# Attention and ResMLP on one core: lam products and beta1 of the first pair on VectorE, and two W1 blocks cast in DRAM beforehand

## The chip, the cores and the metric

The kernel runs on one core of a Trainium2 chip. The metric is device time in microseconds (us) of one execution. An execution that was profiled stands beside the plain runs; its trace gives every instruction's start and duration. Engines are named as in the profile: PE is TensorE (PEld its weight loads), DVE is VectorE, ACT is ScalarE, POOL is GpSimd, SP is SyncE, which here only issues DMAs.

## The reference

Eight batches of 384 tokens. Attention has 16 query heads and 4 key and value heads of 64; its output, laid side by side, is x of width 1024. Then a ResMLP block with affine layers:

```
scores = q k^T / 8 ; attn = softmax(scores) ; x = attn v           (8 x 384 x 1024)
a1  = alpha1 * x + beta1
tok = w_tok @ a1               (384 x 384, over the tokens of a batch)
u   = x + lam * tok
a2  = alpha2 * u + beta2
ch  = relu(a2 @ w_ch1) @ w_ch2         (1024 -> 4096 -> 1024)
out = u + lam * ch
```

All tensors are float32 in DRAM; the matmuls take bfloat16.

## The kernel before

Batches go in four pairs. A pair (`pair`, L772) has two products. The **first product** is a2 times w_ch1, the **second** the hidden layer times w_ch2. Both are done with seven block products in place of eight, in Strassen's manner, numbered o = 1 to 7: sums of blocks of a2 (`sums_a`, L446), of w_ch1 (`sum_w1`, L506) and of w_ch2 (`sum_w2`, L496) are made on VectorE. The w_ch2 sums are made once, during the first pair, and stored to DRAM as bfloat16 (`w2s`, by `keep_w2`, L493, on SP); later pairs fetch them. W1 blocks are loaded anew in every pair by `load_w1` (L181), as casting DMAs from GpSimd's queue into a ring of six slots (`w1`); the same ring holds W2 blocks in the second product. `queue` with `pump` (L534) issues loads in a fixed order as slots come free. `order1` is the order of the W1 blocks, 0, 8, 1, 9, 2, 10 and so on.

While TensorE does the second product of a pair, the attention and token mixing of the next two batches is woven in. `side(b)` (L214) gives these pieces; `put` (L1071) writes into a plan which piece follows which step of which product, and `steps` runs it. A step is a yield of the product, in the second product after every four matmuls. So the order of instructions on each engine is written out by hand. For each of 8 head pairs p of a batch, `side` does scores (L260) and exp (L269), then attention times v with 1/sum and alpha1 on VectorE (L300, L303, L309), then token mixing on TensorE (`tok`, L324), then u = x + tok (L331) and alpha2 (L334) on VectorE. Finally a2 is transposed: in batch 3 and part of others by TensorE (`turn`, L398) with a copy on ScalarE (L400), otherwise by a DMA on SP.

There are two ways of adding beta1. With `fold` (batches 0 to 3) an extra matmul of two stored rows, R and H, is added to every token tile (L328). R and H lie in the memory of the vector `h1` (L97). Without `fold` (batches 4 to 7), VectorE multiplies by alpha1 into a float32 tile `a1f` (L312) and adds lam * beta1 from `h1` (L313). `h1` is set up by `rows4_on` (two memsets on GpSimd, two small loads on SP), `to_all` (a shuffle on VectorE, L1037) and `scale_beta` (a product, L1040), put into the first product of the second pair (steps 20 to 76).

The second product's results are multiplied by lam (`scaled`, L788) and added to the output in DRAM by an accumulating DMA of GpSimd's queue (`store`, L442). The multiplication is L790: on GpSimd for the first pair (`lead`), on VectorE for the others. The first pair's second product is `second_product` (matmuls L752, copies of sums on ScalarE L744 and L764, sums on VectorE L767). Later pairs' first products are L831, their second products L897.

In the first pair, W2 blocks lie for a while in `home(c)` (L468), four places in `arena` that later hold the hidden layer.

Of the kernel before, what the change touches and what calls it, by code (L numbers as in the profile page):

```python
# [13 lines left out]
def kernel(  # L14
# [21 lines left out]
    nc = tc.nc  # L36
    f32 = mybir.dt.float32
    bf = mybir.dt.bfloat16
    EXP = mybir.ActivationFunctionType.Exp
    RELU = mybir.ActivationFunctionType.Relu  # L40
    MUL = mybir.AluOpType.mult
# [8 lines left out]
    P = 128  # L50
    NST = S // P
    NDT = DM // P
# [4 lines left out]
    CW = 2  # L57
    NCH = NNT // CW
    RING = 6
# [21 lines left out]
    w1 = const.tile([P, RING, NDT, CW * P], bf, tag="w1", name="w1")  # L81
# [3 lines left out]
    g1, h1, al2, lam_t = (vecs[:, i] for i in range(4))  # L85
# [10 lines left out]
    turn, a2_turn = [0], [0]  # L96
# [20 lines left out]
    snaps = hTf.bitcast(f32)  # L117
    SLOTS = 7 * NH // 4
    w2s = [tc.dram_tile([P, NDT * CW * P], bf, name=f"w2s{i}") for i in range(SLOTS)]
    PLACE2 = {o: i for i, o in enumerate((1, 2, 6, 5, 3, 7, 4))}  # L120

    def by_tok(ap):
# [53 lines left out]

    w1src = moe_w_ch1.rearrange("(dt di) nf -> di dt nf", di=P)
    w2src = moe_w_ch2.rearrange("(nt ni) d -> ni nt d", ni=P)
    w1_slots, w1_free = {}, list(range(RING))

    def load_w1(c):  # L181
        w1_slots[c] = w1_free.pop(0)
        nc.gpsimd.dma_start(out=w1[:, w1_slots[c]], in_=w1src[:, :, c * CW * P:(c + 1) * CW * P])  # L183

    def bank(shape, tag, name, dtype=f32):
        if tag == "mm":
# [27 lines left out]
    def side(b):  # L214
        vb = vt[b % 2]
        ess, avs, a1s, a2s, xr = {}, {}, {}, {}, {}
        first, fold = b < 2, b < 4
        kT_, qT_ = kTs.get(b, kT), qTs.get(b, qT)

        def x_of(p):  # L220
# [184 lines left out]
        at = {}  # L405

        def put(k, *m):
            at.setdefault(k, []).append(m)
# [3 lines left out]
        for p in range(NP):  # L412
            put((4, 10, 14, 18, 24, 29, 33, 35)[p], av, p)
            put((8, 15, 17, 22, 27, 32, 36, 38 if b % 2 else 39)[p], tok_flip, p)
            if by_pe(p):
                put(((13, 20, 22, 28, 34, 37, 40, 42) if b == 3 else (0, 0, 0, 0, 0, 36, 39, 41))[p], turn, p)
        return at

    def loads(b):
# [19 lines left out]
    order1 = [c for g in range(NCH // 2) for c in (g, g + NCH // 2)]  # L439
# [28 lines left out]
    def home(c):  # L468
        return arena[:, HOME + c * 2048:HOME + (c + 1) * 2048]
# [5 lines left out]
    def stored(c):  # L475
        return w2s[4 * PLACE2[2] + c]

# [26 lines left out]
        free(raw["12", c][0])  # L504

    def sum_w1(g, o):  # L506
        a, c = w1[:, w1_slots[g]], w1[:, w1_slots[g + NCH // 2]]
        H1, H2 = slice(0, NDT // 2), slice(NDT // 2, NDT)
        if o == 7:
            tt(out=c[:, H1], in0=c[:, H2], in1=c[:, H1], op=SUB)  # L510
            tb[g, 7], tb[g, 1], tb[g, 2], tb[g, 3] = c[:, H1], a[:, H1], a[:, H2], c[:, H2]
            return
        tb[g, o] = t = piece().rearrange("p (a c) -> p a c", a=NDT // 2)
        x, y = {5: (c[:, H1], a[:, H1]), 6: (c[:, H2], tb.get((g, 5))), 4: (a[:, H2], tb.get((g, 6)))}[o]
        tt(out=t, in0=x, in1=y, op=SUB)
# [14 lines left out]
    def free(slot):  # L530
        (w1_free if slot < RING else pad_free).append(slot)
        pump()
# [39 lines left out]
    queue = [(load_block, kind, gp) for kind, gp in (("R1", 0), ("R2", 0), ("L1", 1), ("L2", 1), ("R1", 1), ("R2", 1))]  # L572
    queue += [(load_w2, "21", c, w1_free) for c in range(4)]
    for name, cs, slots in (("12", (0, 1), w1_free), ("12", (2, 3), pad_free), ("22", (0,), pad_free), ("22", (1, 2, 3), w1_free),
                            ("again", (0,), w1_free), ("again", (1,), pad_free), ("again", (2, 3), w1_free)):
        queue += [(load_w2, name, c, slots) for c in cs]
    queue += [(load_w1, c) for c in order1[:4]]
    for i in range(1, NB):
        heads = [(load_w1, c) for c in order1[:4]] if i + 1 < NB else []
        queue += [(load_w1, c) for c in order1[4:]] + [(fetch, i, n) for n in range(SLOTS - 2)] + heads[:2]  # L580
        queue += [(fetch, i, n) for n in (SLOTS - 2, SLOTS - 1)] + heads[2:]

    IDENT = mybir.ActivationFunctionType.Identity
# [188 lines left out]
    def pair(i):  # L772
        b0 = 2 * i
        lead = i == 0
# [12 lines left out]

        def scaled(o, b, ms, dw, t):  # L788
            if o != 2 or not last:
                (nc.gpsimd if lead else nc.vector).tensor_tensor(out=t, in0=t, in1=lam_t[:, dw * 512:(dw + 1) * 512], op=MUL)  # L790
            store(b, ms, dw, t)

        def flush(n=9):
# [24 lines left out]
        for g in range(NH // 2):  # L818
            X, Y, snap = {}, {}, {}
            for k, (o, e) in enumerate(SEQ1):  # L820
                t = 2 * g + e
                lo, hi = bias1[:, t:t + 1], bias1[:, NH + t:NH + t + 1]
                if o == 1:
                    X[e] = pairs["X"].tile([P, 512], f32, tag="X", name="X", bufs=2)
                if o == 7:
                    Y[e] = pairs["Y"].tile([P, 512], f32, tag="Y", name="Y", bufs=2)
                if o == 2:
                    Z = pairs["Z"].tile([P, 512], f32, tag="Z", name="Z", bufs=4)
                ps = (X[e] if o in (1, 6, 5, 3) else Y[e] if o in (7, 4) else Z)[:, :S]
                for dt in range(NDT // 2):  # L830
                    nc.tensor.matmul(out=ps, lhsT=tb[g, o][:, dt, e * P:(e + 1) * P], rhs=opb(LEFT1[o])[:, dt],  # L831
                                     start=(o in (1, 2, 7) and dt == 0), stop=(dt == NDT // 2 - 1), skip_group_check=True)
                if o in (1, 6, 5):
                    q = ((2 if g % 2 else 8) + 2 * (1, 6, 5).index(o) + e) % 12 * S
                    snap[o, e] = snaps[:, q:q + S]
                    nc.scalar.activation(out=snap[o, e], in_=ps, func=IDENT, bias=hi if o == 5 else lo)  # L836
                if o == 5:
                    tt(out=hid[:, t, 1], in0=Y[e][:, :S], in1=snap[5, e], op=ADD)  # L838
                elif o == 2:
                    tt(out=hid[:, t, 0], in0=ps, in1=snap[1, e], op=ADD)  # L840
                elif o == 3:
                    nc.scalar.activation(out=hid[:, t, 4], in_=ps, func=RELU, bias=hi)  # L842
                elif o == 4:
                    tt(out=hid[:, t, 2], in0=ps, in1=snap[6, e], op=ADD)
                if k == 7 and 0 < g < 4:
                    flush(1)
                if (o, e) in ((2, 1), (3, 1)):
                    free(w1_slots.pop(g if o == 2 else g + NCH // 2))
                if k == 3 and g == 0:
                    tt(out=opb(6), in0=opb(4), in1=opb(5), op=SUB)  # L850
                if k == 2 and g == 0:
                    sum_w1(0, 4)
                if k in (2, 5, 8, 11) and g + 1 < NH // 2:
                    sum_w1(g + 1, {2: 5, 5: 7, 8: 6, 11: 4}[k])
                ts = slice(2 * g, 2 * g + 2)
                if k == 1 and g:
                    finish(slice(2 * g - 2, 2 * g))
                if (o, e) == (3, 1):
                    nc.scalar.activation(out=hid[:, ts, 1], in_=hid[:, ts, 1], func=RELU)
                if (o, e) == (4, 1):  # L860
                    nc.vector.tensor_scalar(out=hid[:, ts, 2], in0=hid[:, ts, 2], scalar1=0.0, scalar2=None,
                                            op0=mybir.AluOpType.max)
                    tt(out=hid[:, ts, 3], in0=hid[:, ts, 2], in1=hid[:, ts, 1], op=ADD)
                yield 0
# [11 lines left out]
        for k, o in enumerate(PLACE2):  # L876
            whole = not last and o != 4
            tail = last and o == 4
            for h in range(1 if whole else 2):
                for ms in range(NST - (tail and not h)):  # L880
# [37 lines left out]
                    if (whole or h == 1) and not (last and o == 4):  # L918
# [3 lines left out]
                        else:  # L922
                            bb, dw = where[o]
                            t = snap[1, ms] if o == 7 else spare(ms).bitcast(f32)
# [22 lines left out]
    with tc.manual_schedule(engines=order):  # L947
# [123 lines left out]
        def put(ps, phase, at, *m):  # L1071
            plan.setdefault((ps, phase, at), []).append(m)
# [17 lines left out]
        put(0, 0, 8, rows4_on, (3, 0), (3, 1))  # L1090
        put(0, 0, 30, to_all, 3, 0, 0)
        put(0, 0, 34, to_all, 3, 1, 1)
        put(1, 0, 20, rows4_on, (1, 0), (1, 1))
        put(1, 0, 54, to_all, 1, 0, 0)
        put(1, 0, 68, to_all, 1, 1, 1)
        put(1, 0, 62, scale_beta, 0)
        put(1, 0, 76, scale_beta, 1)
        for c in range(4):
            put(0, 0, (50, 72, 74, 44)[c], load_w2, "11", c)
            put(0, 0, (6, 14, 42, 46)[c], cast_w2, "21", c)  # L1100
            put(0, 1, (41, 43, 45, 47)[c], keep_w2, 1, c)
            put(0, 1, 38 + 2 * c, keep_w2, 3, c)
            put(0, 1, (9, 10, 13, 15)[c], sum_w2, 5, c)
            put(0, 1, (20, 21, 25, 26)[c], sums_first_hid, 2, c)
            put(0, 1, (28, 30, 31, 34)[c], sums_first_hid, 4, c)
            put(0, 1, (37, 40, 41, 43)[c], sum_w2, 6, c)
            put(0, 1, (44, 45, 49, 50)[c], sums_first_hid, 3, c)
            put(0, 1, (51, 54, 57, 58)[c], sum_w2, 7, c)
            put(0, 1, (61, 64, 68, 71)[c], last_w2, c)
        for u, o in ((77, 5), (79, 7), (81, 6)):  # L1110
            put(0, 1, u, sum_w1, 0, o)
        for ps in range(NB - 1):
            c = 2 * ps + 2
# [23 lines left out]
        first = steps(0)  # L1137
# [76 lines left out]
```

## Time and profile before

| what | value |
|---|---|
| median of 3 runs | 733.9 us |
| lowest, highest | 733.42, 741.46 us |
| the profiled execution | 731.92 us, its span 729.9 us |
| TensorE busy | 717.4 us (98%), granted clock 1.00 |
| VectorE, ScalarE, GpSimd busy | 543.9, 373.8, 199.2 us |
| moved by DMA | 153.26 MB, mean 210 GB/s |

The span is the time from the first instruction of the trace to the last; the profiled execution's own time is 2.0 us longer. The first pair's first product ends near 128 us, its second product near 234.5 us, and the second pair's first product near 306 us.

How to read the lines: a timeline line is start, duration, engine, line of the kernel, operation, output <- inputs, shape, count, and in brackets how long the engine had been idle before it and what ended that idle. A line of a source view gives minimum, median and maximum duration in ns, and the first and last start. "out<-in" are the program's names: `sc` a PSUM bank of scores or token mixing, `C` an accumulator of the second product, `xr` attention output, `vecs` the vectors lam, alpha and beta, `w` the ring.

### The profile page before, as it was taken

What the parts mean: (1) busy time and instruction counts of PE and PEld (TensorE: products, weight loads), DVE (VectorE), ACT (ScalarE), POOL (GpSimd) and SP (SyncE); (2) the same over time, 40 slices, a digit from 0 to 9 for tenths busy, and PEclk for the clock granted to TensorE, in tenths of its full rate; (3) what the DMA queues carried; (4) which work ended last, traced back from release to release, by engine and by line L of the source; (5) the groups of instructions that cost most, each with busy time, mean ns of one, the idle gap of its engine ahead of it and who ended that gap; (6) DMA issues with size and microseconds to landing.
All of it is one profiled execution on the core that took longest, in us unless ns stands there. A gap on an engine that the chain in (4) does not pass through costs nothing.

```text
span 729.9 us, 14511 instructions
## 1 busy us (share of the span) xinstructions
PE 717.4 (98%) x5716; PEld 408.7 (56%) x5716; DVE 543.9 (75%) x1009; ACT 373.8 (51%) x566; POOL 199.2 (27%) x242
## 2 busy tenths in 40 slices
PE   8899999999999999999999999999999999999998
PEld 4665555555555666555555566655555566654444
DVE  7888876577888988649678888748868988763354
ACT  7877666544563666643433466663333366650000
POOL 8844233221046551201022344200002222000011
PEclk9999999999999999999999999999999999999999
DMA  9999999999999999969989999998989999937965
GB/s 164 180 239 231 190 195 227 226 242 235 366 312 232 179 182 196 234 221 207 272 193 220 160 162 194 212 227 201 270 233 183 210 126 146 165 123 264 302 174 104
DMA packets 197616, 153.26 MB, mean 210 GB/s; under 512 B 90540, under 2 KB 175892, under 8 KB 197292
## 3 DMA queue, kind: packets, MB, share of 16 engines
q0 software_dynamic: 109872, 64.47, 65.4%
q1 hardware_dynamic: 86988, 87.42, 42.8%
q8 instruction: 44, 0.72, 0.4%
q10 hardware_dynamic: 688, 0.46, 0.2%
q14 instruction: 24, 0.20, 0.1%
HBM read 155.23 MB, written 39.85 MB: 267 GB/s over the span
## 4 chain that ended last, share of the span: by engine, by line
PE 90%; DVE 4%; POOL 2%; DMA 1%; issue 1%; ACT 1%; DVEq 0%; ACTq 0%; POOLq 0%
PE C L897 30%; PE X L831 17%; PE C L752 10%; PE Y L831 9%; PE Z L831 4%; PE sc L260 4%; PE X L681 4%; PE sc L295 3%; PE sc L324 3%; PE Y L681 3%; DMA ops<-obuf 1%; DVE pad L565 1%; PE Z L681 1%; PE tok L324 1%; POOL obuf L334 0%
## 5 line engine op out<-in xcount | busy, mean ns | idle before, releaser
L897 PE MATMUL C<-w,arena 128*128 128x512 bf16 (+2 forms) x744 | 168.3, 372 | 0.0
L269 ACT ACTIVATE es<-sc 128x1024 bf16<-128x1024 f32 x108 | 104.1, 1024 | 116.0 <-PE sc L260 107.6
L897 PEld LDWEIGHTS <-arena 128*128 128x128 bf16 x1040 | 94.8, 98 | 100.5 <-issue 5.1
L442 POOL DMA_DIRECT2D out_dram<-hT x45 | 40.0, 888 | 294.7 <-DVE hT L790 135.9
L836 ACT ACTIVATE hT<-X,bias 128x384 f32<-128x384 f32 x144 | 83.6, 582 | 60.0 <-PE X L831 55.2
L831 PEld LDWEIGHTS <-w 128*128 128x128 bf16 x768 | 75.1, 98 | 50.0
L831 PEld LDWEIGHTS <-pad 128*128 128x128 bf16 x576 | 56.4, 98 | 37.2
L183 POOL DMA_DIRECT2D w<-in_moe_w_ch_dram x48 | 45.4, 1002 | 105.6 <-PE X L831 36.5
L831 PE MATMUL X<-ops,w 128*128 128x384 bf16 x384 | 70.3, 326 | 0.0
L831 PE MATMUL X<-ops,pad 128*128 128x384 bf16 x384 | 70.3, 326 | 0.0
L897 PE MATMUL C<-pad,arena 128*128 128x512 bf16 (+2 forms) x296 | 70.2, 373 | 0.0
L324 PEld LDWEIGHTS <-wtokT 128*128 128x128 bf16 x576 | 39.0, 98 | 16.4 <-issue 3.4
L752 PEld LDWEIGHTS <-arena 128*128 128x128 bf16 x336 | 29.8, 98 | 30.0 <-issue 2.5
L331 DVE TENSOR_TENSOR xr<-sc,xr 128x384 f32<-128x384 f32 x48 | 26.5, 553 | 25.6 <-PE sc L324 14.3
L752 PE MATMUL C<-w,arena 128*128 128x512 bf16 x168 | 41.2, 379 | 0.0
L838 DVE TENSOR_TENSOR arena<-Y,hT 128x384 bf16<-128x384 f32 x48 | 26.5, 556 | 17.7 <-ACT hT L836 16.0
L295 PEld LDWEIGHTS <-es 128*128 128x128 bf16 x864 | 32.8, 97 | 11.3
L831 PE MATMUL Y<-ops,w 128*128 128x384 bf16 x192 | 39.1, 326 | 0.0
L831 PE MATMUL Z<-ops,w 128*128 128x384 bf16 x192 | 39.0, 326 | 0.0
L269 ACT ACTIVATE hT<-sc 128x1024 bf16<-128x1024 f32 x36 | 35.8, 1031 | 4.3 <-PE sc L260 4.0
L260 PE MATMUL sc<-qT,kT 64*128 64x384 bf16 (+2 forms) x504 | 37.2, 271 | 0.5 <-ACT hT L269 0.2
L842 ACT ACTIVATE arena<-X,bias 128x384 bf16<-128x384 f32 x48 | 27.9, 582 | 17.7 <-PE X L831 16.1
(190 smaller groups left out, 1175.1 us busy)
## 6 DMA issues: line engine op xcount, KB each, us to landing
w<-w2s SPq DMA_DIRECT2D x67, 512.0 KB, 5.1
w<-in_moe_w_ch_dram POOLq DMA_DIRECT2D x65, 512.0 KB, 9.8
pad<-w2s SPq DMA_DIRECT2D x25, 512.0 KB, 6.9
out_dram<-hT POOLq DMA_DIRECT2D x45, 256.0 KB, 7.1
out_dram<-xr SPq DMA_DIRECT2D x48, 192.0 KB, 5.3
q_raw<-in_q_dram POOLq DMA_DIRECT2D x28, 192.0 KB, 9.5
w2s<-w SPq DMA_DIRECT2D x10, 512.0 KB, 7.6
arena<-in_moe_w_ch_dram POOLq DMA_DIRECT2D x8, 512.0 KB, 15.9
```

The source lines that it names most:

```text
L183: nc.gpsimd.dma_start(out=w1[:, w1_slots[c]], in_=w1src[:, :, c * CW * P:(c + 1) * CW * P])
L260: nc.tensor.matmul(out=sc[:, hh, k % 4:k % 4 + n], lhsT=kT_[r, 2 * p // G, BLK[hh][sk], :], rhs=qT_[r, p, st:st + n, :], start=True, stop= ...
L269: nc.scalar.activation(out=e, in_=sc, func=EXP, scale=scale_qk)
L295: nc.tensor.matmul(out=av[:, hh, sq, :], lhsT=ess[k // 4][:, m % 2, k % 4, :], rhs=vb[:, sk, hk, :], start=(sk == 0), stop=(sk == NST - 1))
L324: nc.tensor.matmul(out=ps[:, tt, :], lhsT=wtokT[:, st, tt * P:(tt + 1) * P], rhs=a1s[p][:, st, :], start=(st == 0), stop=(st == NST - 1 an ...
L442: nc.gpsimd.dma_start(out=by_tok(out[b])[:, ms, dw * 512:(dw + 1) * 512], in_=o, accum_op=ADD)
L681: nc.tensor.matmul(out=ps[:, :n], lhsT=tb[G, o][:, dt, e * P:(e + 1) * P], rhs=opb(FIRST1[o], n)[:, dt], start=(o in (1, 2, 7) and dt == 0 ...
L752: nc.tensor.matmul(out=x, lhsT=lead_hid[:, t, FIRST2[o], ms * P:(ms + 1) * P], rhs=rhs[:, t % 4 * 512:(t % 4 + 1) * 512], start=(o in (1, ...
L831: nc.tensor.matmul(out=ps, lhsT=tb[g, o][:, dt, e * P:(e + 1) * P], rhs=opb(LEFT1[o])[:, dt], start=(o in (1, 2, 7) and dt == 0), stop=(dt ...
L836: nc.scalar.activation(out=snap[o, e], in_=ps, func=IDENT, bias=hi if o == 5 else lo)
L842: nc.scalar.activation(out=hid[:, t, 4], in_=ps, func=RELU, bias=hi)
L897: nc.tensor.matmul(out=x, lhsT=hid[:, t, LEFT2[o], ms * P:(ms + 1) * P], rhs=rhs[:, t % 4 * 512 + c0:t % 4 * 512 + c1], start=((not last o ...
```

## The change

Four edits in one.

1. `fold` holds only for batches 0 and 1. Batches 2 and 3 take the way of L312 and L313. So beta1's preparation moves from the second pair's first product to the first pair's first product: `rows4_on` at step 40, shuffles at 54 and 64, products with lam at 59 and 69.
2. The lam products of the first pair (L790, 12 of them) go from GpSimd to VectorE.
3. Two blocks of the second pair's W1 (`order1[3]` and `order1[4]`) are cast from DRAM to DRAM by GpSimd's queue during the second product (steps 15 and 17), and loaded by SP into `home(0)` and `home(1)` at steps 76 and 77. The ring takes `order1[:3]` there, and the queue goes on with `order1[5:]`.
4. In batch 3 the turn of head pair 2 is put at 23 in place of 22, behind the token mixing of head pair 3.

```diff
+    w1s = [tc.dram_tile([P, NDT * CW * P], bf, name=f"w1s{i}") for i in range(2)]
...
-    w1_slots, w1_free = {}, list(range(RING))
+    w1_slots, w1_at, w1_free = {}, {}, list(range(RING))
...
     def load_w1(c):
         w1_slots[c] = w1_free.pop(0)
-        nc.gpsimd.dma_start(out=w1[:, w1_slots[c]], in_=w1src[:, :, c * CW * P:(c + 1) * CW * P])
+        w1_at[c] = w1[:, w1_slots[c]]
+        nc.gpsimd.dma_start(out=w1_at[c], in_=w1src[:, :, c * CW * P:(c + 1) * CW * P])
+
+    def cast_w1(i, c):
+        nc.gpsimd.dma_start(out=w1s[i].rearrange("p (a c) -> p a c", a=NDT), in_=w1src[:, :, c * CW * P:(c + 1) * CW * P])
+
+    def back_w1(i, c, at):
+        w1_at[c] = at.rearrange("p (a c) -> p a c", a=NDT)
+        nc.sync.dma_start(out=at, in_=w1s[i])
+
+    def free_w1(c):
+        if c in w1_slots:
+            free(w1_slots.pop(c))
...
-        first, fold = b < 2, b < 4
+        first = fold = b < 2
...
-                put(((13, 20, 22, 28, 34, 37, 40, 42) if b == 3 else (0, 0, 0, 0, 0, 36, 39, 41))[p], turn, p)
+                put(((13, 20, 23, 28, 34, 37, 40, 42) if b == 3 else (0, 0, 0, 0, 0, 36, 39, 41))[p], turn, p)
...
-        a, c = w1[:, w1_slots[g]], w1[:, w1_slots[g + NCH // 2]]
+        a, c = w1_at[g], w1_at[g + NCH // 2]
...
-    queue += [(load_w1, c) for c in order1[:4]]
+    queue += [(load_w1, c) for c in order1[:3]]
...
-        queue += [(load_w1, c) for c in order1[4:]] + [(fetch, i, n) for n in range(SLOTS - 2)] + heads[:2]
+        queue += [(load_w1, c) for c in order1[4 if i > 1 else 5:]] + [(fetch, i, n) for n in range(SLOTS - 2)] + heads[:2]
...
-                (nc.gpsimd if lead else nc.vector).tensor_tensor(out=t, in0=t, in1=lam_t[:, dw * 512:(dw + 1) * 512], op=MUL)
+                nc.vector.tensor_tensor(out=t, in0=t, in1=lam_t[:, dw * 512:(dw + 1) * 512], op=MUL)
...
-                    free(w1_slots.pop(g if o == 2 else g + NCH // 2))
+                    free_w1(g if o == 2 else g + NCH // 2)
...
-        put(1, 0, 20, rows4_on, (1, 0), (1, 1))
-        put(1, 0, 54, to_all, 1, 0, 0)
-        put(1, 0, 68, to_all, 1, 1, 1)
-        put(1, 0, 62, scale_beta, 0)
-        put(1, 0, 76, scale_beta, 1)
+        put(0, 0, 40, rows4_on, (1, 0), (1, 1))
+        for i in range(2):
+            put(0, 0, 54 + 10 * i, to_all, 1, i, i)
+            put(0, 0, 59 + 10 * i, scale_beta, i)
...
+        for i, u in enumerate((15, 17)):
+            put(0, 1, u, cast_w1, i, order1[3 + i])
+            put(0, 1, 76 + i, back_w1, i, order1[3 + i], home(i))
```

In the second and later pairs the W1 blocks of a pair come as before.

## The prediction

> **What bounds the kernel now.** I read the page first, for who is busy, then the busy time by stretch, then TensorE's own timeline for the places where it stands still, and last the VectorE and GpSimd timelines around those places.
>
> ```profile
> PE 717.4 (98%) x5716; PEld 408.7 (56%) x5716; DVE 543.9 (75%) x1009; ACT 373.8 (51%) x566; POOL 199.2 (27%) x242
> ```
> ```profile
> 128.00:200.00 72.00, 72.00 (x692) 40.14 (x691) 52.00 (x82) 38.47 (x51) 13.30 (x13) 1.00 1.12 265
> 200.00:235.00 35.00, 33.22 (x299) 18.48 (x298) 31.23 (x49) 18.19 (x29) 16.68 (x16) 1.00 1.15 280
> 235.00:306.00 71.00, 71.00 (x439) 42.76 (x437) 57.46 (x102) 47.50 (x80) 31.44 (x38) 1.00 1.38 191
> ```
>
> TensorE is busy 717.4 of 729.9 us, at a granted clock of 1.00, so 12.5 us of stall is all there is beyond taking matmuls away. Columns of the stretches: length, then busy time of PE, PEld, DVE, ACT, POOL, clock, DMA share, GB/s. 128 to 235 us is the first pair's second product, which carries attention and token mixing of batches 2 and 3; 235 to 306 is the next pair's first product. TensorE loses 1.78 us in 200 to 235 and nothing in the two neighbours. There VectorE is 31.23 of 35 busy, and GpSimd is busiest too.
>
> ```profile
> 204.89 0.33 PE L324 MATMUL sc<-a,wtokT 128*128 128x128 bf16 x3 [0.59 <-ACT es L269]
> ...
> 221.20 0.33 PE L398 MATMUL sc<-ident,obuf 128*128 128x128 bf16 x3 [0.24 <-ACT es L269]
> ...
> 224.76 0.34 PE L324 MATMUL sc<-a,wtokT 128*128 128x128 bf16 x3 [0.95 <-DVE a L309]
> ```
>
> These three idles are the 1.78 us. The last waits for VectorE's alpha1 product of one head pair.
>
> ```profile
> 212.16 0.56 DVE L331 TENSOR_TENSOR xr<-sc,xr 128x384 f32<-128x384 f32 x1 [0.77 <-PE sc L328]
> 212.75 1.77 DVE L334 TENSOR_TENSOR obuf<-xr,vecs 128x384 bf16<-128x384 f32 x1
> ...
> 220.87 2.02 DVE L499 TENSOR_TENSOR w<-w,pad 128x2048 bf16<-128x2048 bf16 x1
> ...
> 225.44 1.74 DVE L309 TENSOR_TENSOR a<-xr,vecs 128x384 bf16<-128x384 f32 x1
> ```
> ```profile
> 212.82 1.28 POOL L790 TENSOR_TENSOR hT<-hT,vecs 128x512 f32<-128x512 f32 x1
> ...
> 220.24 1.55 POOL L790 TENSOR_TENSOR hT<-hT,vecs 128x512 f32<-128x512 f32 x1
> ...
> 225.19 1.56 POOL L790 TENSOR_TENSOR hT<-hT,vecs 128x512 f32<-128x512 f32 x1
> ```
>
> L334 and L309 usually take 0.56 us and L499 1.22. Whenever one overlaps a lam product on GpSimd (L790) it ends about when that product ends: 1.77, 2.02, 1.74 us. Each such meeting costs VectorE 0.4 to 1.2 us.
>
> ```profile
> L328 PE MATMUL sc<-vecs x48: 218/219/219, 138.3 to 227.9; 128*128 128x128 bf16 x48
> ...
> L312 DVE TENSOR_TENSOR a1f<-xr,vecs x32: 557/558/561, 313.9 to 572.7; 128x384 f32<-128x384 f32 x32
> L313 DVE TENSOR_TENSOR a<-a1f,vecs x32: 557/557/559, 314.5 to 573.3; 128x384 bf16<-128x384 f32 x32
> ...
> 238.07 0.69 DVE L515 TENSOR_TENSOR pad<-w 128x1024 bf16<-128x1024 bf16 x1 [2.92 <-DMA w<-in_moe_w_ch_dram]
> ```
>
> The 48 matmuls of L328 go away. L312 and L313 show, from batches 4 to 7, what comes instead. The last line is the wait that the two early casts address: 2.92 us of VectorE, while TensorE is 71.00 of 71 busy.
>
> **The change, part by part.**
>
> *beta1 on VectorE.* Removed: 48 matmuls (L328). Pipelined they are 0.055 us apart: a token group of 12 starts at 138.12 and is followed at 138.79 (0.67 us), one of 9 without them in a later pair at 317.23 and 317.73 (0.50). So 16 x 0.17 = 2.7 us leave TensorE, all of it on the path. Added: 16 VectorE operations; a pair L312, L313 starts 0.59 apart, so 16 x 0.59 = 9.4 us. VectorE has 20.0 us idle in 128 to 200, and I followed its queue there: the operand is ready 1.0 to 2.9 us ahead of its token matmuls for batch 2 still. It costs nothing there except at one place (step 53, near 197 us), where it was just in time: 0.2 us.
>
> *beta1's preparation moved* from the next pair's first product into the first pair's. On VectorE two shuffles of 0.72 (L1037) and two products of 512 columns (0.68, L790's VectorE rows). Two of the four fall in VectorE idles of 2.1 to 2.2 us ahead of L693 and cost nothing; without that cover they would cost their 0.6. Two fall ahead of L702, which frees a Y bank: it ended about 91.6 us where TensorE took the bank at 91.98, 0.4 us to spare against 0.6 added. So 0.25 each, 0.5 in all (bounds 0 and 1.4, their whole time). Two memsets on GpSimd (1.11 us for both) and two 8 KB DMAs on SP move along, into a 5.8 us idle of GpSimd; nobody behind them is near its due time.
>
> *lam products on VectorE.* Twelve of 0.68, queued 0.61 apart: three by 165 us, six in 212 to 230, three beside the next product. GpSimd's queue then holds only stores and loads. Against the six, 3.7 us, stand the meetings that end: 1.21 (L334), 0.37 and 0.52 (L309), 0.80 (L499), 1.18 (L309), together 4.1 us. The Trainium skill ("SBUF — State Buffer", Who interferes with whom) says that a VectorE instruction with two SBUF inputs is blocked by a GpSimd instruction that reads SBUF, not by one that only writes it, and infers that making DMA descriptors needs the write side alone. By that, what stays on GpSimd's queue would hold VectorE nowhere, and the sum is as below; were the stores to hold it too, as in the second rival, it would come out at 735.0. The trace bears the first half (L331, with one PSUM input, is never over 0.56 in 200 to 235); the second half it leaves open.
>
> *VectorE in 204 to 235.* At 204.10 its L499 waits for the landing of a W2 store, which itself hangs on SP's stores, issued without a break from 183 to 206 at 360 to 376 GB/s. TensorE is 1.1 us ahead by then (1.6 less the 0.5 above), but that train is set by DMA, so I take a landing at 203.5, between 203.0 (all shifted) and 204.1 (unmoved). From there the work to the next product's sums was 25.2 us, with 2.0 of idle and 4.1 of meetings: 19.1 of work. Add 4 x 0.58 for beta1, 5 x 0.61 for products, and about 0.2 of waits for ScalarE that stay: 24.6, so the first W1 sum starts at 228.1 (before 229.27). The sums up to the last opb(0) took 5.3 us, one product among them makes 5.9: 234.0. TensorE wants opb(0) for its fifth group of the new product (o=7) at 235.68 in the old count; with 2.7 + 0.6 + 0.2 saved (the last two below), less 0.5 for the preparation and 0.5 for three small waits on VectorE (0.2 above, 0.2 near 208, 0.1 near 224), it would be there at 233.2. It waits 0.8 us: a new stall in a place that had none (bounds 0 and 1.4, by the landing).
>
> *turn of pair 2 of batch 3 one step later.* The 0.59 us at 204.89 is the second score bank being emptied; the turn that took the first bank ahead of it is moved behind it, so the token group takes the bank that is free first: minus 0.6 (bounds 0 and 0.6). The 0.95 at 224.76 falls to about 0.75, the 0.24 stays.
>
> *W1 casts.* Two blocks (order1[3] and [4]) are cast by GpSimd's queue near 146 and 152 us and come back by SP near 225. A cast of this kind is in the trace (w2s<-in_moe_w_ch_dram): 10.2 to 18.7 us to landing; a load back (w<-w2s) 5.1. The back load lands near 231, before VectorE's use, so the 2.92 us go and VectorE is in step again after its late start. TensorE was not waiting, so this gains nothing by itself; without it VectorE's lag would meet the load's. Danger: W2 loads issued at 158.5 to 160.7 follow the casts on one queue and landed at 164.3, 169.5 and 173.4 (three in 14.9 us, 5 each); TensorE uses the last at 176.9. At 5 us each the casts are gone by 157.5: zero; at 10.2 the loads slip by 4. I take zero, as nothing else is in that queue then. The Trainium skill ("DMA: Bandwidth & Descriptors", Anatomy of one DMA) fits 2.0 us plus bytes over 436 GB/s; an estimate by it for 1 MB read is 4.4 us, also gone in time. The trace's 10.2 says such casts run slower than that.
>
> **Sum.** 2.7 + 0.6 + 0.2 gained; 0.5 (preparation), 0.5 (small waits) and 0.8 (opb(0)) lost: 1.7 us. The profiled execution took 731.92 (span 729.9), 2.0 under the median of 733.9; so 730.2 in its terms, and **732.2 us** against the median.
>
> **The rivals.**
> - *VectorE keeps up.* The store lands at 203.0 or before, and there is no wait at opb(0), at the small places or at 224.76 (0.95): 2.7 + 0.6 + 0.95 less 0.5 = 3.75, 730.1 us. For it: VectorE idles 5 us in 186 to 212. Against: it is 31.23 of 35 busy behind that.
> - *VectorE becomes the bound and it is slower.* Landing unmoved at 204.1 and each of some 14 added operations 0.1 dearer than by its queue distance (0.68, not 0.61), or GpSimd's stores and loads (0.9 us each) still holding VectorE: opb(0) at 236 to 237, past 235.7. That is the point of decision; beyond it the first product starts later than now although 2.7 us of matmuls are gone: 735.0. For it: 95% busy in 220 to 230. Against: the 4.1 us of meetings must then not come back.
> - *The casts delay the W2 loads.* At 10.2 us the last block lands at 177.4 where TensorE, 0.7 ahead (seven token groups, 1.2, less 0.5), wants it at 176.2: 1.2 us of new idle, of which the 0.8 at opb(0) may come back: 732.6 to 733.4. At 18.7, seen where four other loads were in the queue, the loads would slip by 13 and cost ten: for that the queue is too empty here.
> - *The casts do not shorten VectorE's wait* because SP issues the back loads behind a token spill that waits for VectorE: no change of the time, as TensorE is full in 235 to 306; it lies inside the forecast.
>
> **Chances.** Forecast 0.60, its own range 731.0 to 733.6 (turn 0 to 0.6, preparation 0 to 1.4, landing 203.0 to 204.1). VectorE keeps up 0.17; VectorE bound 0.14; casts late 0.09. The range of 8 in 10 reaches into both sides: 729.6 to 735.8. 2% of 733.9 is 14.7 us, about what a measurement of this kernel can tell from no change; no case reaches that: faster by over 2% 0.01, within 0.97, slower 0.02.
>
> **What would show it.** TensorE busy about 714.7, no L328 rows after 128 us; no VectorE L334, L309 or L499 over 1.3 us near 212 to 227; a TensorE idle of about 1 us in front of Y of the first product's o=7, released by VectorE's L449; the 0.59 gone; the 2.92 gone. It is wrong if TensorE idles in 128 to 200, if the new idle is over 3 us, or if W2 blocks arrive late at 175.

## The result, and the profile after

| | before | after |
|---|---|---|
| median | 733.42 us (17 runs) | 741.71 us (17 runs) |
| lowest, highest | 731.02, 742.48 us | 738.23, 748.91 us |
| ratio after / before | | 1.0109, interval 1.0083 to 1.0136 |
| the profiled execution, its span | 731.92, 729.9 us | 742.97, 741.2 us |

The changed kernel is slower by 1.1%. The prediction, 732.2 us with a range of 729.6 to 735.8, was wrong: the time lies 8 us above the median of before. A ratio compares the fast runs of both kernels and is not the quotient of the medians. The two profiled executions are 11.1 us apart where the medians are 8.3 apart, so what the two traces show adds up to more than the loss. In the kernel after, lines stand 13 further down than before (the matmul L324 is L337, the product L309 is L325 and L326, the load L183 is L185).

Busy time in the page of after, and then its busy time by stretch (columns as in the prediction: length, PE, PEld, DVE, ACT, POOL, clock, DMA share, GB/s):

```profile
PE 722.0 (97%) x5668; PEld 407.6 (55%) x5668; DVE 550.4 (74%) x1037; ACT 374.1 (50%) x566; POOL 181.4 (24%) x230
```
```profile
128.00:200.00 72.00, 68.02 (x609) 36.17 (x608) 52.62 (x88) 36.99 (x48) 9.33 (x12) 0.95 1.22 236
200.00:235.00 35.00, 32.09 (x290) 17.06 (x288) 29.75 (x51) 17.66 (x27) 5.25 (x6) 0.95 1.14 316
235.00:306.00 71.00, 68.83 (x422) 40.53 (x422) 57.12 (x108) 42.84 (x73) 23.48 (x28) 1.00 1.35 193
```

The 48 matmuls are gone (5716 to 5668), and yet TensorE is busy for 4.6 us more. Where it was busy for 72.00 of 72, it is now busy for 68.02, and the granted clock is 0.95: a busy TensorE that runs slower does less. The DMA share (packet times added up over the engines, so it can pass 1) rose from 1.12 to 1.22 while the rate fell from 265 to 236 GB/s. So 128 to 200 us, which the prediction took for safe, is where the time goes first. TensorE's timeline of after names the waits:

```profile
178.79 0.61 PE L273 MATMUL sc<-qT,kT 64*128 64x256 bf16 x4 [2.03 <-DVE xr L316]
180.44 0.61 PE L273 MATMUL sc<-qT,kT 64*128 64x128 bf16 x4 [1.04 <-DVE xr L344]
214.33 1.02 PE L765 MATMUL C<-arena 128*128 128x512 bf16 x4 [1.73 <-DVE arena L512]
...
232.64 0.68 PE L337 MATMUL sc<-a,wtokT 128*128 128x128 bf16 x9 [0.73 <-DVE a L326]
...
248.57 1.46 PE L844 MATMUL X<-ops,pad 128*128 128x384 bf16 x8 [1.93 <-ACT hT L849]
```

Four of these five idles are new; 232.64 is the old one of 224.76, 0.73 for 0.95. With a wait for a W2 block at 175.41 (0.91), TensorE loses 5.9 us from 170 to 216 where before lost 0.6. VectorE's timeline of after says what VectorE itself waited for in two of them:

```profile
178.17 0.56 DVE L316 TENSOR_TENSOR xr<-sc,rinv 128x384 f32<-128x384 f32 x1 [4.46 <-DMA out_dram<-xr]
...
213.05 1.23 DVE L512 TENSOR_TENSOR arena<-pad,arena 128x2048 bf16<-128x2048 bf16 x1 [2.07 <-DMA w2s<-arena]
```

At 178.17 it wants to write a new `xr`. There are four `xr` buffers, and the oldest is still being read by the token store (`spill`, L227 before), which puts x + lam * tok into the output. Counted by the four buffers, it is the store that SP issued at 162.60 (157.44 in before): 5.2 us later, and its buffer came free only 15.6 us after the issue. SP issues in order, and that store stands behind DMA transposes of a2. So the next view is SP's timeline: two of the transposes of a2 of before, then two of after (the second column is the time that SP takes to issue one). From 140 to 192 us, eight each, it was 1.23 to 2.73 us in before and 1.26 to 5.77 in after; the last line of each view is the slowest.

```profile
156.11 1.23 SPq L337 DMA_TRANSPOSE ops<-obuf  x1
...
170.72 2.73 SPq L337 DMA_TRANSPOSE ops<-obuf  x1
```
```profile
157.54 4.97 SPq L350 DMA_TRANSPOSE ops<-obuf  x1
...
169.53 5.77 SPq L350 DMA_TRANSPOSE ops<-obuf  x1
```

And the DMA issues from 140 to 190 us, first before, then after; the last number is the median time to landing:

```profile
w<-in_moe_w_ch_dram POOLq DMA_DIRECT2D x3, 512.0 KB, 9.6
...
ops<-obuf SPq DMA_TRANSPOSE x8, 3.5
```
```profile
w<-in_moe_w_ch_dram POOLq DMA_DIRECT2D x3, 512.0 KB, 15.8
w1s<-in_moe_w_ch_dram POOLq DMA_DIRECT2D x2, 512.0 KB, 15.0
...
ops<-obuf SPq DMA_TRANSPOSE x7, 14.4
```

The two casts (`w1s`) take 13.8 and 16.2 us (the line has the median). Beside them SP's transposes, which stand in another queue, land four times later, 14.4 for 3.5 us. The Trainium skill ("DMA: Bandwidth & Descriptors", Issuing engines are not separate DMA queues) says that DMAs started by different engines run on the same 16 DMA engines and interleave there. The 14.4 for 3.5 agrees with that. SP reaches its train of W2 stores at 188.19, not at 178.67, and the wait of L512 at 213.05 is for one of these stores.

The idles can cost more than their length. In the stretch 180 to 185 of after, right behind two of them:

```profile
180.00:185.00 5.00, 4.56 (x21) 2.23 (x21) 3.18 (x6) 2.66 (x4) 0.00 (x0) 0.51 1.36 146
```

The granted clock is 0.51 (0.80 in 175 to 180, 0.66 in 215 to 220; before it is 1.00 in all three). Five microseconds at 0.80, 0.51 and 0.66 are 1.0, 2.5 and 1.7 us of full speed lost, 5.2 at most, since part of that time was idle anyway. Not every idle does this: behind the 1.93 us at 248.57 the clock stayed at 1.00. When the next pair's first product begins, TensorE is at 242.0 us; before it was at 234.4. When that pair's second product begins it is 10.3 us behind (317.5 for 307.2), the 1.93 at 248.57 among them.

### The profile page after: what moved, and what is told of

It is laid out like the page before. It is cut to its first block, busy times and chain, and to the rows that moved or that the text cites. A ratio compares the mean times of both kernels' runs of the same rounds, so it can differ in the third digit from the quotient of the medians.

```text
span 741.2 us, 14418 instructions
## 1 busy us (share of the span) xinstructions
PE 722.0 (97%) x5668; PEld 407.6 (55%) x5668; DVE 550.4 (74%) x1037; ACT 374.1 (50%) x566; POOL 181.4 (24%) x230
## 4 chain that ended last, share of the span: by engine, by line
PE 79%; DVE 8%; DMA 6%; issue 3%; POOL 2%; ACT 2%; SPq 0%; DVEq 0%; POOLq 0%; ACTq 0%
PE C L910 29%; PE X L844 13%; PE Y L844 7%; PE C L765 6%; PE sc L273 4%; PE Z L844 3%; PE X L694 3%; PE sc L308 3%; PE sc L337 3%; PE Y L694 2%; DMA out_dram<-xr 2%; DMA w<-in_moe_w_ch_dram 2%; PE E L626 1%; DMA w2s<-arena 1%; PE av L308 1%
## 5 line engine op out<-in xcount | busy, mean ns | idle before, releaser
L844 PEld LDWEIGHTS <-w 128*128 128x128 bf16 x736 | 72.0, 98 | 48.4 <-issue 0.5
L185 POOL DMA_DIRECT2D w<-in_moe_w_ch_dram x46 | 44.0, 1007 | 101.6 <-DVE xr L316 41.8
L844 PE MATMUL X<-ops,w 128*128 128x384 bf16 x368 | 67.3, 326 | 0.0
L337 PEld LDWEIGHTS <-wtokT 128*128 128x128 bf16 x576 | 38.0, 99 | 16.7 <-issue 3.7
L273 PE MATMUL sc<-qT,kT 64*128 64x384 bf16 (+2 forms) x504 | 38.8, 278 | 3.5 <-DVE xr L316 2.0
L308 PEld LDWEIGHTS <-es 128*128 128x128 bf16 x864 | 32.8, 97 | 11.3
L844 PE MATMUL Y<-ops,w 128*128 128x384 bf16 x184 | 37.6, 326 | 0.3 <-DVE arena L857 0.3
L844 PE MATMUL Z<-ops,w 128*128 128x384 bf16 x184 | 37.4, 326 | 0.0
L855 ACT ACTIVATE arena<-X,bias 128x384 bf16<-128x384 f32 x48 | 27.9, 582 | 17.8 <-PE X L844 16.2
## 6 DMA issues: line engine op xcount, KB each, us to landing
w<-in_moe_w_ch_dram POOLq DMA_DIRECT2D x63, 512.0 KB, 10.3
```

The lines of the kernel that those rows point to most:

```text
L185: nc.gpsimd.dma_start(out=w1_at[c], in_=w1src[:, :, c * CW * P:(c + 1) * CW * P])
L273: nc.tensor.matmul(out=sc[:, hh, k % 4:k % 4 + n], lhsT=kT_[r, 2 * p // G, BLK[hh][sk], :], rhs=qT_[r, p, st:st + n, :], start=True, stop= ...
L308: nc.tensor.matmul(out=av[:, hh, sq, :], lhsT=ess[k // 4][:, m % 2, k % 4, :], rhs=vb[:, sk, hk, :], start=(sk == 0), stop=(sk == NST - 1))
L337: nc.tensor.matmul(out=ps[:, tt, :], lhsT=wtokT[:, st, tt * P:(tt + 1) * P], rhs=a1s[p][:, st, :], start=(st == 0), stop=(st == NST - 1 an ...
```

## The experiments

The theory that the trace of after suggests: the casts' DMA work slows what SP issues, and the late token stores and W2 stores stop VectorE and then TensorE. Rivals: the new work on VectorE (beta1, lam products) makes it late, and the casts only come on top; or the casts cost their share of DMA time wherever they stand, whichever wait shows it. (Where an expectation names theories by letters, what each says of the kernel stands beside the letter.) The first four kernels take the change apart. Each ratio is to runs of before on the same chip, whose median was 733.61 us beside the first four kernels, 733.04 beside the next four that were run (unused casts, earlier casts, no token stores of batch 2, mended order) and 734.14 beside the last four. Each trace is one execution, which can lie off its kernel's median.

**After without the casts (edit 3 undone).**

```diff
-    queue += [(load_w1, c) for c in order1[:3]]
+    queue += [(load_w1, c) for c in order1[:4]]
...
-            put(0, 1, u, cast_w1, i, order1[3 + i])
-            put(0, 1, 76 + i, back_w1, i, order1[3 + i], home(i))
```

> Both casts and their loads back undone; beta1 and lam products on VectorE stay. Theory A (the two casts hold up SP's transposes and token spills, so VectorE waits 5.2 us for xr buffers near 170 to 178 and TensorE stalls with it): those waits go, 733 to 735 us against 733.4 before; the wait of the next product's first copies on ScalarE for late output stores (about 2 us of TensorE idle) stays. Theory B (VectorE carries too much in the first pair's second product): nothing much changes, 739 to 742.

736.3 us, ratio 1.0045 (1.0013 to 1.0077). So without the casts 0.6 of the 1.1% come back. The waits for `xr` are gone, and of those for W2 stores 0.24 us are left on VectorE, as the casts' theory has it. But one large idle is new, in TensorE's timeline and then in VectorE's:

```profile
243.29 2.74 PE L843 MATMUL X<-ops,w 128*128 128x384 bf16 x8 [5.25 <-DVE ops L862]
```
```profile
241.67 0.69 DVE L527 TENSOR_TENSOR pad<-w 128x1024 bf16<-128x1024 bf16 x1 [7.50 <-DMA w<-in_moe_w_ch_dram]
```

VectorE waits 7.50 us for a W1 block. The sum of `ops` (L862) that TensorE needs at once stands behind that waiting instruction. The trace suggests why the block is late: GpSimd's queue is in order as well. The last output store of the first pair now waits for VectorE's lam product and is issued at 230.79, and the three W1 loads behind it go out together at 231.36. Before, the first of them was issued at 232.10, alone, and VectorE had its block 6.0 us later (238.07); here it took 10.3, and 8.2 in two kernels below that issue the same three together.

**The casts alone (before plus edit 3).**

```diff
...
+            put(0, 1, u, cast_w1, i, order1[3 + i])
+            put(0, 1, 76 + i, back_w1, i, order1[3 + i], home(i))
```

> Only the casts and loads back are added to the kernel before. Theory A: 738 to 741 us, with transposes of a2 landing after 10 us and more, an xr wait on VectorE of some us, and TensorE idle near 173 to 180. Theory B: the same as before, 733 to 734.

740.42 us, ratio 1.0089 (1.0051 to 1.0127). Nearly the whole loss is here, with nothing new on VectorE. It waits for a token store, and TensorE for it, in VectorE's timeline and then in TensorE's:

```profile
179.34 0.56 DVE L316 TENSOR_TENSOR xr<-sc,rinv 128x384 f32<-128x384 f32 x1 [6.25 <-DMA out_dram<-xr]
```
```profile
179.95 0.39 PE L273 MATMUL sc<-qT,kT 64*128 64x256 bf16 x4 [3.87 <-DVE xr L316]
```

The rival that VectorE's new work is the main cause falls. The parts do not add up, though: 0.9% for the casts and 0.45% for the rest are more than the 1.1% of both.

**beta1 on VectorE alone (before plus edits 1 and 4).**

```diff
...
-        first, fold = b < 2, b < 4
+        first = fold = b < 2
...
```

> Only beta1 of batches 2 and 3 on VectorE, with its preparation moved and the one turn later. Theory A: 730.5 to 732.5 us, the 2.7 us of matmuls less 0.4 us of the preparation. Theory B: 735 to 737, VectorE late at the start of the next product.

737.43 us, ratio 1.0064 (1.0026 to 1.0102). The two VectorE operations that replace the matmuls, with the lam products still on GpSimd, in VectorE's timeline of the profiled execution, the fastest of its 12 runs (733.58 us, so it does not hold the whole loss of the median):

```profile
213.66 2.54 DVE L324 TENSOR_TENSOR a1f<-xr,vecs 128x384 f32<-128x384 f32 x1
216.23 2.46 DVE L325 TENSOR_TENSOR a<-a1f,vecs 128x384 bf16<-128x384 f32 x1
```

Each takes 0.56 us elsewhere. TensorE waits 3.21 us for L325 at 218.75. GpSimd's lam products end at 215.78 and 218.26, and the two operations 0.42 and 0.43 us behind them (216.20, 218.69): each was held by the product that it overlaps, the first although it began 0.54 us ahead of its product, which the trace does not explain. That is the meeting which the prediction priced, now with twice as many operations to meet.

**lam products on VectorE alone (before plus edit 2).**

```diff
-                (nc.gpsimd if lead else nc.vector).tensor_tensor(out=t, ...)
+                nc.vector.tensor_tensor(out=t, ...)
```

> Only the lam products of the first pair moved to VectorE. Theory A: 733 to 736 us: GpSimd no longer holds VectorE (4.1 us back), but the products stand in VectorE's queue behind the sums, the last store is issued late and ScalarE's first copy of the next product waits 1 to 3 us for it. Theory B: 736 to 738, from VectorE's own load.

736.38 us, ratio 1.0019 (0.9988 to 1.0049): no difference shown. The wait of the first kernel is there in small: VectorE 5.41 us for a W1 block at 239.94, TensorE 2.42 behind it.

Now the casts. Is it their DMA work, or that the blocks come another way?

**Before plus two casts that nobody reads.**

```diff
+            put(0, 1, u, cast_w1, i, order1[3 + i])
```

> The kernel before with the two casts added at their places and nothing else: W1 is loaded as before and the cast blocks are never read, so this is DMA work alone. Theory A (the casts' own traffic slows the transposes that SP issues, SP falls behind, token spills are late, xr buffers stay taken): 738 to 741 us, TensorE idle 3 to 5 us near 175 to 181 and a released-by-DMA wait of 4 to 6 us on VectorE. Rival (the loads back, or the shorter ring order, are what costs): as before, 733 to 735.

741.01 us, ratio 1.01 (1.0063 to 1.0137): the full loss, from the casts as DMA work alone. In VectorE's timeline the same wait, and one of the waits for W2 stores:

```profile
175.66 0.56 DVE L307 TENSOR_TENSOR xr<-sc,rinv 128x384 f32<-128x384 f32 x1 [3.14 <-DMA out_dram<-xr]
...
208.03 1.23 DVE L503 TENSOR_TENSOR arena<-pad,arena 128x2048 bf16<-128x2048 bf16 x1 [3.16 <-DMA w2s<-arena]
```

Here the wait for `xr` is not what costs most. TensorE idles 1.08 us behind it near 177 (0.41 and 0.67). It idles 0.65 and 1.53 us at 209 and 212 for W2 sums that wait for stores, and 1.16 and 1.98 us at 199.38 and 231.87 for VectorE's `a` (before has one such wait, 0.95).

**After, with the casts 50 us earlier,** in the first product.

```diff
-        for i, u in enumerate((15, 17)):
-            put(0, 1, u, cast_w1, ...)
+        for i, u in enumerate((56, 60)):
+            put(0, 0, u, cast_w1, ...)
```

> The changed kernel, its two casts issued at steps 56 and 60 of the first pair's first product (near 100 us) instead of steps 15 and 17 of its second product. Theory A: no transpose is issued by SP in the stretch from there to 130 us, so the stall near 175 goes and 734 to 737 us come out, with the idle ahead of the next product's second half (1.9 us, ScalarE waiting for output stores) left. Rival (such casts cost wherever they stand, by holding GpSimd's queue and the key and value loads behind them): 739 to 742, or a new idle near 130 us.

740.56 us, ratio 1.0076 (1.0042 to 1.011). The theory in its narrow form, a collision in that one stretch, fails, and the result fits the rival by which the casts cost their share anywhere. (After without the casts has 1.0045, and the two intervals overlap.) The casts, issued at 93.7 and 100.5, took 21.7 and 25.3 us, and everything behind them on GpSimd's queue moved: the loads of q went out at 119.9 for 115.3 us, a W2 load at 132.3 for 124.2. TensorE idles at other places (1.62 us at 170.06 for `xr`, 1.04 at 211.86 for a W2 sum, 1.67 at 244.10). By stretch, the DMA share of before is 1.23, 1.46 and 1.24 in 90 to 110, 110 to 128 and 128 to 150 us, and 0.86 only in 155 to 160. So the earlier place was no emptier than the first, and a quiet stretch was not tried.

**The casts alone, without the token stores of batch 2.**

```diff
-            if not first:
+            if not first and b != 2:
                 spill(p)
```

> As e2 (casts and loads back alone), leaving out the stores of x + lam tok of batch 2 to the output, so that its result lacks them. Theory A by way of the xr buffers: VectorE's wait of 6.25 us for a store and TensorE's idle of 3.9 us near 180 go, 734 to 736 us. If TensorE is instead held by late W2 blocks or transposes, most of the 6 us stays: 737 to 740.

735.51 us, ratio 1.0021 (0.9992 to 1.0051). The `xr` wait is gone, and TensorE's 3.87 with it. That speaks for the chain over SP's queue and the four buffers; but these stores also moved 1.6 MB, and only the kernel after the next parts the two. (Left out are batch 2's values of x + lam * tok in the output.)

**One unused cast in place of two.**

```diff
-        for i, u in enumerate((15, 17)):
+        for i, u in enumerate((15,)):
```

> The kernel before with one of the two casts alone, at the first of the two places (issued near 145 us), its block never read. Theory C (the DMA engines have little slack between 95 and 185 us, and the cost is a threshold: a transpose on SP's queue that lands late makes the spills behind it late, but four xr buffers absorb about 4 us of lateness): SP's transposes near 153 to 165 us are slowed to 2 to 4 us and not to 5, SP reaches its first W2 store after 165 us some 2 to 4 us later than the 178.67 of before (two casts: 185.6), TensorE idles under 1.5 us near 177, and the time is 0 to 3 us above before. Rival (each cast costs its share, whatever waits): half of the 7 to 8 us of the run with both casts unused, 3.5 to 4 us, with about half of each of its idles.

737.21 us for 734.14 of before, ratio 1.005 (1.0021 to 1.008), half of the loss with two: 0.5% for 1.0%. The interval, 1.5 to 5.9 us, holds both expectations, so the time does not decide between a threshold (theory C) and a share for each cast. In the trace the four buffers did absorb the lateness, as theory C has it: no `xr` wait is left. But TensorE still loses time at another wait, which theory C did not have:

```profile
178.60 1.25 PE L756 MATMUL C<-w,arena 128*128 128x512 bf16 x4 [1.88 <-DMA w<-in_moe_w_ch_dram]
```

**The casts alone, with the token stores of batches 2 and 3 on ScalarE's queue.**

```diff
-            nc.sync.dma_start(out=by_tok(out[b])[:, :, cols(p)], in_=x_of(p))
+            (nc.scalar if b in (2, 3) else nc.sync).dma_start(out=by_tok(out[b])[:, :, cols(p)], in_=x_of(p))
```

> The run with the casts alone (before plus edit 3), with the token stores of x + lam * tok of batches 2 and 3 issued from ScalarE's queue in place of SP's; nothing is left out. The run without these stores left them out, so it took away both their place behind the transposes and their 1.6 MB. If the place in SP's order is what matters (theory C), the xr wait near 179 us (6.25 on VectorE, 3.87 on TensorE) goes here as well, and the time is 735 to 737.5 against 740.4 with the casts alone. If it is their bytes, the stores are late here too: the wait stays at 3 us or more and the time at 739 or more. Either way ScalarE now waits for VectorE's sum before each store, which can delay an exp by up to 1 us each.

737.94 us, ratio 1.0065 (1.0034 to 1.0096); with the casts alone it was 1.0089 (1.0051 to 1.0127), so a gain is not shown. All stores are made, from a queue with no transposes in it, and the `xr` wait is gone. So the place in SP's order did cause that wait. But another comes up behind it, in TensorE's timeline:

```profile
180.47 1.87 PE L765 MATMUL C<-w,arena 128*128 128x512 bf16 x4 [2.69 <-DMA w<-in_moe_w_ch_dram]
```

The W2 blocks, issued on GpSimd's queue behind the casts, now hold TensorE up, 2.69 us. In the run without the token stores, with 1.6 MB less moved, that wait was 0.46. This looks like two chains, one behind the other: whoever takes away one meets the other. The control below limits that.

**Control: before with these stores on ScalarE's queue.** The same edit as above.

> Control for the former: the kernel before with the token stores of batches 2 and 3 on ScalarE's queue, nothing else. Theory C: before has no xr wait, so there is nothing to win; 733 to 735, with the small waits for es (ScalarE's exp) up by 0 to 2 us in all. A rival in which ScalarE's queue is dear: 736 or more, with TensorE idle behind es.

733.36 us, ratio 0.9996 (0.9964 to 1.0029): the move by itself costs and gains nothing. Its profiled execution was the longest of its ten, with a span of 738.9, and it has nearly the same idle with no cast at all:

```profile
184.22 1.02 PE L752 MATMUL C<-w,arena 128*128 128x512 bf16 x4 [2.51 <-DMA w<-in_moe_w_ch_dram]
```

In it SP's transposes of a2 landed after 10.0 us and the W2 blocks after 15.7 (medians, 140 to 190 us), at a DMA share of 1.17 and 1.23 in 155 to 160 and 160 to 165. So a long execution without casts can show the same lateness; why this one was late was not followed. That the casts cost time rests on the medians of the casts alone and of the unused casts, and no single trace proves which wait they work through.

Last: does the saving of beta1 come back when the W1 wait is kept from spreading?

**After without the casts, VectorE's order mended.** The sum that TensorE needs first (`opb(6)`) is made ahead of the next W1 sums, and these go to the last four places of that group, in the second pair's first product.

```diff
-                if k == 3 and g == 0:
+                if k == 2 and g == 0:
                     tt(out=opb(6), in0=opb(4), in1=opb(5), op=SUB)
-                if k == 2 and g == 0:
                     sum_w1(0, 4)
-                if k in (2, 5, 8, 11) and g + 1 < NH // 2:
-                    sum_w1(g + 1, {2: 5, 5: 7, 8: 6, 11: 4}[k])
+                late_ks = i == 1 and g == 0
+                if k in ((10, 11, 12, 13) if late_ks else (2, 5, 8, 11)) and g + 1 < NH // 2:
+                    sum_w1(g + 1, (5, 7, 6, 4)[k - 10] if late_ks else {2: 5, 5: 7, 8: 6, 11: 4}[k])
```

> As e1 (no casts, beta1 and lam products on VectorE), but opb(6) is made ahead of the W1 sums of the next column group, and these four sums stand at the last four places of the first group instead of spread over it. If the 5.25 us of idle in e1 came from opb(6) standing in VectorE's queue behind a sum that waits 7.5 us for a late W1 block, then most of it goes: 730 to 733 us. If the block's lateness holds TensorE by itself, 734 to 737.

733.37 us for 733.04, ratio 1.0005 (0.997 to 1.0039). TensorE has no idle near 240 us, and the largest one left in 165 to 260 is the one foreseen in the prediction:

```profile
222.30 0.68 PE L336 MATMUL sc<-a,wtokT 128*128 128x128 bf16 x9 [0.73 <-DVE a L325]
```

The profiled execution took 730.15 us, the fastest of its 12; its span is 728.3, 1.6 under before's. The next pair's first product begins at 231.7 (234.4 before) and its second at 305.4 (307.2). So in the trace beta1 gains 2.7 us by 232 us, of which 1.8 are left at 305. In the medians no gain over before is shown: 1.6 us are 0.2%, and the interval is 0.7% wide.

**The same, with the token stores on ScalarE's queue** (the edit of above besides).

> The version with beta1 and lam products on VectorE, no casts, and the mended order of the W1 sums (a span of 728.3 and a ratio of 1.0005 [0.997, 1.0039] to before), with the token stores of batches 2 and 3 on ScalarE's queue besides. If SP's queue still holds a store of W2 sums or a transpose up in this version, 0.5 to 1.5 us come back and it is the first to beat before beyond the noise: 731 to 733. If what is left is not SP's order, 733 to 735, or more by ScalarE's waits.

734.62 us for 734.14, ratio 1.0013 (0.9982 to 1.0045), no difference shown. Its profile has a wait of 1.84 us for ScalarE's exp at 221.14, which stands behind such a store on ScalarE.

## Why the prediction was wrong, point by point

- **The casts: wrong, and the main loss.** The step that failed: "At 5 us each the casts are gone by 157.5: zero; at 10.2 the loads slip by 4. I take zero, as nothing else is in that queue then." They took 13.8 and 16.2 us, past the 10.2 of the upper case and short of the 18.7 that was read and set aside because "the queue is too empty here"; the second landed at 168.1, not at 157.5. The queue was not empty, and it was not the only place to look. In before it held two output stores, issued at 144.37 and 150.09, which took 8.3 and 5.0 us, and the DMA engines that it shares with SP were loaded (the last but one number is their share):

```profile
150.00:155.00 5.00, 5.00 (x49) 2.54 (x47) 4.27 (x8) 1.12 (x2) 0.89 (x1) 1.00 1.17 218
155.00:160.00 5.00, 5.00 (x49) 2.94 (x48) 2.30 (x5) 2.90 (x4) 0.91 (x2) 1.00 0.86 245
160.00:165.00 5.00, 5.00 (x58) 2.92 (x56) 3.85 (x6) 3.33 (x4) 2.10 (x3) 1.00 1.08 154
```

Over these 15 us SP's queue took 0.56 of the share, with transposes and stores, and GpSimd's 0.47. The casts alone cost 1.0089 (6.5 us); unread they cost 1.01 (7.3 us). The term zero measured some 7 us. Two of the prediction's own signs of being wrong came: TensorE idles in 128 to 200, and a W2 block is late at 175.
- **The rival "the casts delay the W2 loads": its mechanism was there, but as the smaller part.** It gave 1.2 us of idle, and 0.91 is there at 175.41. It missed the other queue: late transposes, late token stores, `xr` not free, 2.03 and 1.04 us of TensorE, then the late W2 stores, 1.73.
- **The clock: missed.** The sum took a microsecond of idle for a microsecond. The granted clock fell to 0.51 and 0.66 behind these idles, which is up to 5.2 us of the trace.
- **"The 2.92 us go": right, and replaced.** That wait is gone in after. In its place TensorE waits 1.93 us at 248.57 for `hT`: the last output store, behind a lam product on VectorE, lands late, and ScalarE may not write its buffer before.
- **"GpSimd's queue then holds only stores and loads": right, but priced at nothing.** The stores now wait for VectorE, and the loads behind them wait along. Without the casts that costs 5.25 us of TensorE, with the lam products alone 2.42. In after, where two of the blocks come another way, this wait is not there. The rival "VectorE becomes the bound" gave 735.0 for VectorE's work; it was not the work but one waiting instruction with an urgent one behind it.
- **The meetings with GpSimd: right.** In after no L347, L326 or L512 takes over 1.3 us. Left on GpSimd, the products hold the new pair for 2.54 and 2.46 us. The prediction read that a held operation ends about when the product does; by its lines L334 and L309 end 0.4 us behind it and L499 1.1. What it left open, whether the stores on GpSimd's queue hold VectorE too, the trace of after answers: L512 at 226.09 took its usual 1.22 us beside a store that GpSimd issued from 226.47 to 227.38.
- **beta1's 2.7 us on TensorE, the 0.6 of the turn, the 0.95 that falls to 0.75: right.** 0.59 is gone, 0.73 is left. The version without casts and in the mended order begins the next product 2.7 us earlier; 2.7 + 0.6 + 0.2, less 0.45 for the preparation and 0.43 for one wait for `xr` at 208.19, is 2.6.
- **The preparation, "0.25 each, 0.5 in all": right.** Two idles behind L715, of 0.20 and 0.22 us, at 111.15 and 101.36.
- **The new wait at opb(0), 0.8: not there**, neither in after nor in the version with the mended order.

Left open: whether any transfer of this size costs the same here, or a cast from DRAM to DRAM more than another; only the casts were tried. Open too is how the loss divides among the waits for `xr`, for W2 stores and for W2 blocks, which the traces show in different shares. About 1 us of the 11.3 between the two spans falls behind 317 us (10.3 there), and was not followed.

## What to carry to other kernels

A queue with little in it does not make a transfer free: look at the share of the DMA engines in that stretch, and at what the other queues have due there. For each queue that issues in order, ask what stands behind a late transfer, up to the buffer that is not given back; when one such chain is cut, the next may be just behind it. When a product moves to another engine, its stores move in time too, and with them every load behind them on the same queue. And before a wait in one trace is called the cause, compare that execution's time with the median of its kernel.

## What the runs showed of the hardware

- A cast of one 512 KB block (as written) from DRAM to DRAM took 13.8 and 16.2 us beside other traffic in one stretch of after, 13.2 with one cast in place of two, and 21.7 and 25.3 where the casts stood 50 us earlier.
- The granted clock fell to 0.80 and 0.51 in the ten microseconds that hold idles of 2.03 and 1.04 us, and to 0.66 behind one of 1.73 and 0.20. It stayed at 1.00 behind 1.93 in the same trace, and behind 1.98 with the unused casts, so the length alone does not say it. The Trainium skill ("TensorE: Matmul & The Clock Gate", What's actually happening) gives half the clock after an idle window of about 3.4 us. The 0.51 agrees with the half; the idles here were shorter than that window, and some were enough.
- SP itself took from 1.23 to 2.73 us to issue a transpose of a2 in before and up to 5.77 in after, and for a transpose of q 4.51 in before and 8.50 with one cast. It issued nothing else meanwhile, so a transpose can hold up its queue already at the issue.
